# A list scheduler takes other engines' results to reach TensorE by a fixed margin later, and its costs are set anew

## Chip, core and metric

One core of a Trainium2 chip runs the whole program. The metric is the device time in microseconds of one execution.

## What is computed

Three stages follow each other on 2304 tokens (4 batches of 576): attention that keeps each row's 32 largest scores, an MLP with the gate h·cos(h), and a mixture of eight experts that all see every token and whose outputs are weighted by a matrix P, balanced in eight rounds.

```python
scores = scale * np.matmul(q, k.transpose(0, 1, 3, 2))
kth = np.partition(scores, -32, axis=-1)[..., -32:-31]
attn = softmax(np.where(scores >= kth, scores, -1e9)); x = attn @ v
h = x @ w_in; x = (h * np.cos(h)) @ w_out
P = exp(x @ w_gate); eight times: rows of P to sum 1, then columns, times N / E
out += P[:, e:e + 1] * (np.maximum(x @ w1[e], 0.0) @ w2[e])     # for each of 8 experts
```

w_in and w_out arrive as 64-bit numbers and are decoded on the core to 32-bit ones.

## The kernel before

Nothing is issued where it is written. Each `put` (L262) records an operation with its engine, a cost in ns, what it reads and writes, and a priority by engine and class of work (`PRIORITY`, L28). `Plan.issue` (L150) then runs a list scheduler: it keeps a time at which each engine is free, takes the earliest engine that has something ready, and gives it the ready operation with the smallest priority number. An operation is ready when all that it depends on has ended, plus a latency by the two engines (`LAT`, L75). The order in which operations are taken is the order in which they are issued, so the table of costs decides where every instruction stands in its engine's queue. Each engine then works through its queue strictly in that order and waits, where an input is late, with all that stands behind.

The work, in the order of the program:

- *Decode*: 32 blocks of weights. Per block two VectorE (DVE) operations (L325, L331), four ScalarE (ACT) and three GpSimd (POOL) ones (L330, L332, L333) that hand the data back and forth, and a transfer in and out.
- *First attention* and *first MLP*: 3 token tiles of batch 0, in plain fp32, beside the decode. An attention tile (`att_tile`, L436) is 128 rows of one head: scores in two halves through the one PSUM bank s (L447, L448, or L451 in the plain form), each copied out by ACT (L457); on DVE one MAX8 (L459), three rounds of MATCH_REPLACE8 and MAX8 (L464, L465) and a masked product (L466); small POOL operations (L460, L468, L470); then transposes of the weights `ex` on TensorE (PE) into the bank t, four and then one (L475), evacuated by ACT and DVE (L493, L494). Per head `att_out` multiplies by v (L501, L503), again in bank t. The third tile's gate (L588 to L595) leads to `x2fl` (L669), without which the experts' work can't start.
- *Attention* of all other tokens (batch 0, 1, 2, 3), whose buffers come free with the end of the decode, beside *fill*: the experts' two layers (`fill`, L762) for the 3 first tiles, later for 4 more. On PE attention has priority 2 and fill 3, so fill goes where attention is not ready.
- *moe1*: the first MLP for the other tokens, one part (512 tokens) after batch 1, three parts after batch 3.
- P (`sinkhorn`), then the experts for the other tokens, with products combined in pairs; to the end.

fp32 products are made of three matmuls of rounded parts (`mm3`, L370: high·high, high·low, low·high), so weights are split into `whi` and `wlo` on ACT and POOL (L345, L347).

Of the kernel before, what the change touches and what calls it, by code (L numbers as in the profile page):

```python
# [12 lines left out]
I32 = mybir.dt.int32  # L13
U32 = mybir.dt.uint32
AF = mybir.ActivationFunctionType
ALU = mybir.AluOpType
# [7 lines left out]
LOWEST = -3.0e38  # L24
# [12 lines left out]
class Buf:  # L37


    def __init__(self, plan, pool, shape, dtype, name):  # L40
        self.plan, self.pool, self.shape, self.dtype, self.name = plan, pool, shape, dtype, name
        self.tile = None
        self.log = []
# [27 lines left out]
class Plan:  # L71
# [6 lines left out]
        ("POOL", "ACT"): 69.0, ("POOL", "DVE"): 70.0, ("POOL", "POOL"): 96.0, ("PE", "SP"): 189.0, ("ACT", "SP"): 140.0,  # L78
        ("DVE", "SP"): 120.0, ("POOL", "SP"): 67.0, ("SP", "SP"): 10.0, ("SP", "PE"): 80.0, ("SP", "ACT"): 10.0, ("SP", "DVE"): 10.0, ("SP", "POOL"): 10.0,
    }  # L80

    def __init__(self, tc, pools):
        self.tc, self.pools = tc, pools
# [66 lines left out]
    def issue(self):  # L150
        ops = self.ops
        for op in ops:
            op.outs, op.left, op.ready = [], len(op.deps), 0.0
        for k, op in enumerate(ops):
            for d in op.deps:
                ops[d].outs.append(k)
        engines = ("PE", "ACT", "DVE", "POOL", "SP")
        soon = {e: [] for e in engines}
        now = {e: [] for e in engines}
        free = dict.fromkeys(engines, 0.0)  # L160
        dma_free, func, warm, window, busy = 0.0, None, False, -1, {}
        for k, op in enumerate(ops):
            if not op.left:
                heapq.heappush(soon[op.eng], (0.0, k))
        order = []
        while len(order) < len(ops):
            best = None
            for e in engines:
                if now[e]:
                    t = free[e]  # L170
                elif soon[e]:
                    t = max(free[e], soon[e][0][0])
                else:
                    continue
                if best is None or t < best[0]:
                    best = (t, e)
            t, e = best
            while soon[e] and soon[e][0][0] <= t:
                k = heapq.heappop(soon[e])[1]
                heapq.heappush(now[e], (ops[k].prio, k))  # L180
            k = heapq.heappop(now[e])[1]
            op = ops[k]
            cost = op.cost
            if op.func and op.func != func:
                cost, func = cost + 1283.0, op.func
            if e == "PE":
                w = int(t / 3413)
                if w != window:
                    past = busy.get(w - 1, 0.0) / 3413
                    warm = past > 0.95 or (warm and past > 0.5)  # L190
                    window = w
                cost *= 1.0 if warm else 2.0
                a = t
                while a < t + cost:
                    z = min(t + cost, (int(a / 3413) + 1) * 3413.0)
                    busy[int(a / 3413)] = busy.get(int(a / 3413), 0.0) + z - a
                    a = z
            free[e] = op.end = t + cost
            if e == "SP":
                dma_free = max(t + cost + 650.0, dma_free) + op.bytes / 360.0  # L200
                op.end = dma_free + 900.0
            order.append(k)
            for o in op.outs:
                n = ops[o]
                n.ready = max(n.ready, op.end + self.LAT.get((e, n.eng), 130.0))
                n.left -= 1
                if not n.left:
                    heapq.heappush(soon[n.eng], (n.ready, o))
        self.estimate = max(op.end for op in ops)
        for k in order:  # L210
            ops[k].emit()


def mm_ns(n):
    return max(107.0, n / 2.4 + 3.0)


def act_ns(n, psum=False, ap=False):
# [11 lines left out]
def fused_kernel(tc, kq, vv, w_in, w_out, w_gate, w1, w2, out, B=4):  # L230
# [4 lines left out]
    V, A_, G_, T_ = nc.vector, nc.scalar, nc.gpsimd, nc.tensor  # L235
# [26 lines left out]
    def put(eng, cost, emit, reads=(), writes=(), func=None, nbytes=0):  # L262
        return add(eng, cost, emit, reads, writes, PRIORITY[eng][CLASSES.index(work)], func, nbytes)
# [51 lines left out]
    def decode(src, keep, part):  # L315

        raw, mag, sgn, low = d_raw(), d_mag(), d_sgn(), d_low()  # L320
        dma(lambda: raw.ap, lambda: src.bitcast(I32), 1 << 19, writes=[raw])
        hi = lambda dt: raw.ap.bitcast(dt).rearrange("p (n t) -> p n t", t=2)[:, :, 1]
        lo = lambda: raw.ap.bitcast(U32).rearrange("p (n t) -> p n t", t=2)[:, :, 0]
        magf = lambda: mag.ap.bitcast(F32)
        put("DVE", 335, lambda: V.tensor_scalar(mag.ap, hi(I32), 3, 0x40000000, op0=ALU.logical_shift_left, op1=ALU.bitwise_xor), [raw], [mag])  # L325
        put("ACT", 613, lambda: A_.activation(sgn.ap, hi(F32), AF.Identity, bias=cols.ap[:, 1:2]), [raw, cols], [sgn])
        put("ACT", 613, lambda: A_.activation(sgn.ap, sgn.ap, AF.Sign, bias=cols.ap[:, 2:3]), [sgn, cols], [sgn])
        put("ACT", 520, lambda: A_.activation(low.ap, lo(), AF.Copy, scale=2.0**-52), [raw], [low])
        put("ACT", 520, lambda: A_.activation(magf(), magf(), AF.Abs), [mag], [mag])
        put("POOL", 1225, lambda: G_.tensor_tensor(magf(), magf(), sgn.ap, op=ALU.mult), [mag, sgn], [mag])  # L330
        put("DVE", 335, lambda: V.tensor_scalar(sgn.ap.bitcast(I32), mag.ap, -8388608, None, op0=ALU.bitwise_and), [mag], [sgn])  # L331
        put("POOL", 1225, lambda: G_.tensor_tensor(low.ap, low.ap, sgn.ap, op=ALU.mult), [low, sgn], [low])  # L332
        put("POOL", 1225, lambda: G_.tensor_tensor(low.ap, magf(), low.ap, op=ALU.add), [mag, low], [low])  # L333
        dma(keep, lambda: low.ap, 1 << 18, [low], [part])
# [101 lines left out]
    def att_tile(stats, dests, plain=None):  # L436
# [4 lines left out]
        sc, m, wk, ex = sc_r(), m_r(), wk_r(), ex_r()  # L441
# [16 lines left out]
        mc = lambda i, k=1: m.ap[:, i : i + k]  # L458
# [2 lines left out]
        put("ACT", act_ns(S, ap=True), lambda: A_.activation(ex.ap, sc.ap, AF.Exp, scale=0.125, bias=mc(32)), [sc, (m, 32, 33)], [ex], func="exp")  # L461
        for r in range(3):
            src = wk if r else sc
            put("DVE", 669, lambda r=r, src=src: V.match_replace(wk.ap, mc(8 * r, 8), src.ap, LOWEST), [src, (m, 8 * r, 8 * r + 8)], [wk])  # L464
            put("DVE", 669, lambda r=r: V.max(mc(8 * r + 8, 8), wk.ap), [wk], [(m, 8 * r + 8, 8 * r + 16)])  # L465
        put("DVE", 729, lambda: V.scalar_tensor_tensor(ex.ap, sc.ap, mc(31), ex.ap, op0=ALU.is_ge, op1=ALU.mult, accum_out=mc(33)),  # L466
            [sc, ex, (m, 24, 32)], [ex, (m, 33, 34)])
        put("POOL", 162, lambda: G_.tensor_scalar(mc(34), mc(33), 1e-9, 1.0, op0=ALU.add, op1=ALU.mult), [(m, 33, 34)], [(m, 34, 35)])  # L468
        put("DVE", 75, lambda: V.reciprocal(mc(35), mc(34)), [(m, 34, 35)], [(m, 35, 36)])  # L469
# [2 lines left out]
        for c0, c1, p in ((0, 4, 128), (4, 5, 64)):  # L472
# [8 lines left out]
            for r0, rn, hd, t0 in dests:  # L481
# [10 lines left out]
                hi, lo = (ath, 1000 * c0 + t0, 1000 * c0 + t0 + rn), (lb, 2000 * c0 + t0, 2000 * c0 + t0 + rn)  # L492
# [601 lines left out]
```

## Time and profile before

| | us |
|---|---|
| median of 3 runs (lowest, highest) | 2482.4 (2480.8, 2483.6) |
| the profiled execution | 2480.5 |
| its span, first to last instruction | 2478.7 |

The profile is of one execution. Its records give start and duration of each instruction; the page says that matmuls are pipelined and their ends modelled, so that the record of one overlaps the next. PEld is TensorE's loading of weights, which stands ahead of each matmul. A wait is the engine's idle time and the instruction that ended it. Row names in the fences further down are lines of the kernel before.

### The profile page before, as it was taken

What the parts mean: (1) busy time and instruction counts of PE and PEld (TensorE: products, weight loads), DVE (VectorE), ACT (ScalarE), POOL (GpSimd) and SP (SyncE); (2) the same over time, 40 slices, a digit from 0 to 9 for tenths busy, and PEclk for the clock granted to TensorE, in tenths of its full rate; (3) what the DMA queues carried; (4) which work ended last, traced back from release to release, by engine and by line L of the source; (5) the groups of instructions that cost most, each with busy time, mean ns of one, the idle gap of its engine ahead of it and who ended that gap; (6) DMA issues with size and microseconds to landing.
All of it is one profiled execution on the core that took longest, in us unless ns stands there. A gap on an engine that the chain in (4) does not pass through costs nothing.

```text
span 2478.7 us, 33516 instructions
## 1 busy us (share of the span) xinstructions
PE 2364.7 (95%) x11089; PEld 1905.7 (77%) x11089; DVE 1986.9 (80%) x3651; ACT 1271.7 (51%) x2438; POOL 1266.6 (51%) x1328
## 2 busy tenths in 40 slices
PE   6878999999889999999999999999999999999999
PEld 3434688888667877778878888788888888888887
DVE  8997599999998999999986787776666666666655
ACT  6785566666578666666566776322322222322221
POOL 6886487767577656656520033433443334443330
PEclk9889999999899999999999999999999999999999
DMA  8765654444323333333334333022222221111101
GB/s 263 232 210 186 200 167 144 139 123 151 109 74 97 114 115 115 115 119 97 97 114 123 91 108 104 27 64 81 81 85 81 73 60 35 36 42 43 35 22 47
DMA packets 159501, 261.37 MB, mean 105 GB/s; under 512 B 15008, under 2 KB 60656, under 8 KB 159328
## 3 DMA queue, kind: packets, MB, share of 16 engines
q1 hardware_dynamic: 159328, 259.24, 34.5%
q8 instruction: 87, 1.43, 0.2%
q14 instruction: 86, 0.70, 0.1%
HBM read 227.31 MB, written 31.87 MB: 105 GB/s over the span
## 4 chain that ended last, share of the span: by engine, by line
PE 57%; DVE 28%; POOL 6%; issue 4%; ACT 3%; DMA 1%; SPq 0%; POOLq 0%; ACTq 0%; DVEq 0%
PE y L372 9%; PE y L373 9%; PE y L374 9%; DVE wk L464 7%; DVE m L465 6%; DVE ex L466 4%; PE g L374 2%; PE g L373 2%; PE g L372 2%; DVE m L459 2%; POOL wlo L347 2%; DVE atl L494 1%; PE y L383 1%; PE y L387 1%; PE y L384 1%
## 5 line engine op out<-in xcount | busy, mean ns | idle before, releaser
L347 POOL TENSOR_TENSOR wlo<-raw,whi 128x512 fp32r<-128x512 f32 x336 | 451.7, 1349 | 195.1 <-ACT whi L345 116.3
L465 DVE MAX8 m<-wk 128x8 f32<-128x576 f32 x432 | 318.1, 748 | 1.9
L953 DVE SCALAR_TENSOR_TENSOR acc<-y,P,acc 128x512 f32<-128x512 f32 x308 | 229.2, 748 | 103.5 <-PE y L374 103.2
L345 ACT ACTIVATE whi<-raw 128x512 fp32r<-128x512 f32 x416 | 259.2, 627 | 96.5 <-PE y L374 36.9
L464 DVE MATCH_REPLACE8 wk<-m,wk 128x576 f32<-128x576 f32 x288 | 213.5, 742 | 1.1
L372 PE MATMUL y<-whi,gh 128*128 128x512 f32 x448 | 182.0, 406 | 0.0
L372 PE MATMUL y<-gh,xh 128*128 128x512 f32 x450 | 177.1, 393 | 1.0 <-DVE acc L949 1.0
L374 PE MATMUL y<-whi,gl 128*128 128x512 f32 x448 | 176.5, 394 | 0.0
L373 PE MATMUL y<-gl,xh 128*128 128x512 f32 x450 | 176.5, 392 | 0.0
L374 PE MATMUL y<-gh,xl 128*128 128x512 f32 x450 | 176.2, 392 | 0.0
L373 PE MATMUL y<-wlo,gh 128*128 128x512 f32 x448 | 176.0, 393 | 0.0
L475 PE MATMUL t<-ident,ex 128*128 128x128 f32 (+1 forms) x720 | 136.6, 290 | 39.7 <-POOL ex L470 10.9
L457 ACT ACTIVATE sc<-s 128x288 f32<-128x288 f32 x288 | 117.0, 406 | 95.6 <-DVE ex L466 54.9
L475 PEld LDWEIGHTS t<-ident,ex 128*128 128x128 f32 (+1 forms) x720 | 85.9, 140 | 101.6 <-POOL ex L470 27.8
L466 DVE SCALAR_TENSOR_TENSOR ex<-sc,m,ex 128x576 f32<-128x576 f32 x144 | 152.8, 1061 | 3.6 <-ACT ex L461 1.8
L470 POOL TENSOR_SCALAR ex<-ex,m 128x576 f32<-128x576 f32 x144 | 111.2, 772 | 33.9 <-DVE m L469 33.0
L493 ACT ACTIVATE ath<-t 64x128 fp32r<-64x128 f32 (+3 forms) x272 | 104.5, 396 | 46.2 <-PE t L475 40.0
L461 ACT ACTIVATE ex<-sc,m 128x576 f32<-128x576 f32 x144 | 111.3, 773 | 32.4 <-POOL m L460 31.4
L459 DVE MAX8 m<-sc 128x8 f32<-128x576 f32 x144 | 106.9, 743 | 9.2 <-ACT sc L457 9.1
L464 DVE MATCH_REPLACE8 wk<-m,sc 128x576 f32<-128x576 f32 x144 | 106.7, 741 | 0.0
L372 PEld LDWEIGHTS y<-gh,xh 128*128 128x128 f32 x450 | 85.2, 189 | 20.0 <-DVE acc L949 1.8
L372 PE MATMUL y<-gh,gh 128*128 128x512 f32 x254 | 99.4, 391 | 0.0
(376 smaller groups left out, 7054.6 us busy)
## 6 DMA issues: line engine op xcount, KB each, us to landing
raw<-in_w_dram SPq DMA_DIRECT2D x384, 256.0 KB, 2.6
kq<-in_kq_dram SPq DMA_DIRECT2D x32, 576.0 KB, 4.3
raw<-win_d SPq DMA_DIRECT2D x64, 256.0 KB, 3.0
raw<-wout_d SPq DMA_DIRECT2D x64, 256.0 KB, 2.7
y_d<-st SPq DMA_DIRECT2D x56, 256.0 KB, 3.0
raw<-y_d SPq DMA_DIRECT2D x56, 256.0 KB, 2.7
wp<-win_d SPq DMA_DIRECT2D x24, 512.0 KB, 5.3
wp<-wout_d SPq DMA_DIRECT2D x24, 512.0 KB, 4.4
```

The source lines that it names most:

```text
L345: put("ACT", act_ns(n), lambda: A_.activation(hv(), rv(), AF.Copy), [rb], [hb])
L347: put(e, c, lambda: f.tensor_tensor(lv(), rv(), hv().bitcast(F32), op=ALU.subtract), [rb, hb], [lb])
L372: T_.matmul(o(), ah(), bh(), start=start, stop=False)
L373: T_.matmul(o(), ah(), bl(), start=False, stop=False)
L374: T_.matmul(o(), al(), bh(), start=False, stop=stop)
L457: put("ACT", act_ns(288, psum=True), lambda c=c: A_.activation(sc.ap[:, c], o(), AF.Copy), [ps_s], [(sc, c.start, c.stop)])
L459: put("DVE", 669, lambda: V.max(mc(0, 8), sc.ap), [sc], [(m, 0, 8)])
L464: put("DVE", 669, lambda r=r, src=src: V.match_replace(wk.ap, mc(8 * r, 8), src.ap, LOWEST), [src, (m, 8 * r, 8 * r + 8)], [wk])
L465: put("DVE", 669, lambda r=r: V.max(mc(8 * r + 8, 8), wk.ap), [wk], [(m, 8 * r + 8, 8 * r + 16)])
L466: put("DVE", 729, lambda: V.scalar_tensor_tensor(ex.ap, sc.ap, mc(31), ex.ap, op0=ALU.is_ge, op1=ALU.mult, accum_out=mc(33)), [sc, ex, (m, ...
L475: T_.transpose(pt()[:p, c - c0, :], ex.ap[:, c * 128 : c * 128 + p], ident.ap)
L953: put("DVE", 663, lambda y=y, av=av, pcol=pcol: V.scalar_tensor_tensor(av(), y.ap, pcol(), av(), op0=ALU.mult, op1=ALU.add), [y, P, a], [a])
```

## The change

A constant `SLACK` of 600 ns is added to the time at which PE can take a result of another engine or of a transfer, in the planner's estimate only. The transfer rate of the estimate goes from 360 to 280 bytes per ns, a matmul's cost from n / 2.4 + 3.0 to n / 2.4 + 13.6 ns, and five DVE costs are raised. No operation, buffer, priority or wait is added or removed; only the order of issue differs. Lines of the new kernel are 4 higher than those of the kernel before.

```diff
+    SLACK = 600.0
...
             if e == "SP":
-                dma_free = max(t + cost + 650.0, dma_free) + op.bytes / 360.0
+                dma_free = max(t + cost + 650.0, dma_free) + op.bytes / 280.0
                 op.end = dma_free + 900.0
...
                 n = ops[o]
-                n.ready = max(n.ready, op.end + self.LAT.get((e, n.eng), 130.0))
+                n.ready = max(n.ready, op.end + self.LAT.get((e, n.eng), 130.0) + (self.SLACK if n.eng == "PE" != e else 0.0))
...
 def mm_ns(n):
-    return max(107.0, n / 2.4 + 3.0)
+    return max(107.0, n / 2.4 + 13.6)
...
-        put("DVE", 335, lambda: V.tensor_scalar(mag.ap, hi(I32), 3, 0x40000000, op0=ALU.logical_shift_left, op1=ALU.bitwise_xor), [raw], [mag])
+        put("DVE", 600, lambda: V.tensor_scalar(mag.ap, hi(I32), 3, 0x40000000, op0=ALU.logical_shift_left, op1=ALU.bitwise_xor), [raw], [mag])
...
-            put("DVE", 669, lambda r=r, src=src: V.match_replace(wk.ap, mc(8 * r, 8), src.ap, LOWEST), [src, (m, 8 * r, 8 * r + 8)], [wk])
+            put("DVE", 738, lambda r=r, src=src: V.match_replace(wk.ap, mc(8 * r, 8), src.ap, LOWEST), [src, (m, 8 * r, 8 * r + 8)], [wk])
...
-        put("DVE", 729, lambda: V.scalar_tensor_tensor(ex.ap, sc.ap, mc(31), ex.ap, op0=ALU.is_ge, op1=ALU.mult, accum_out=mc(33)),
+        put("DVE", 960, lambda: V.scalar_tensor_tensor(ex.ap, sc.ap, mc(31), ex.ap, op0=ALU.is_ge, op1=ALU.mult, accum_out=mc(33)),
```

(The decode's second DVE operation, L331, goes from 335 to 600 as the first does.)

What this does to the queues is shown at three places. The first is PE's queue in the second stretch of attention and fill, between a tile's last transpose (`t<-ident,ex`, 64x128) and the product with v (`t<-ath,vs`), which needs that transpose evacuated by ACT and DVE. Before:

```order
L475 MATMUL t<-ident,ex_223 64x128
L372 MATMUL g<-x2fh,whi_1687 128x512
L373 MATMUL g<-x2fl,whi_1687 128x512
L374 MATMUL g<-x2fh,wlo_1715 128x512
L372 MATMUL g<-x2fh,whi_1687 128x512
L373 MATMUL g<-x2fl,whi_1687 128x512
L374 MATMUL g<-x2fh,wlo_1715 128x512
L501 MATMUL t<-ath_1604,vs_1393 128x320
```

And now:

```order
L479 MATMUL t<-ident,ex_236 64x128
L376 MATMUL g<-x2fh,whi_1749 128x512
L377 MATMUL g<-x2fl,whi_1749 128x512
L378 MATMUL g<-x2fh,wlo_1764 128x512
L376 MATMUL g<-x2fh,whi_1749 128x512
L377 MATMUL g<-x2fl,whi_1749 128x512
L378 MATMUL g<-x2fh,wlo_1764 128x512
L376 MATMUL g<-x2fh,whi_1749 128x512
L377 MATMUL g<-x2fl,whi_1749 128x512
L378 MATMUL g<-x2fh,wlo_1764 128x512
L505 MATMUL t<-ath_1605,vs_1193 128x320
```

Three matmuls of fill more stand between the two. Over all such places of this stretch the product stands 10 rows behind (median of 27 places) before, 7 rows in 9 of them; now 12 rows (median of 26), 7 rows in one.

The second place is DVE's queue ahead of the first MLP's third gate (L590, now L594). Before:

```order
L669 TENSOR_TENSOR x2fl<-y_754,x2fh 128x4x128
L459 MAX m_127<-sc_115 128x8
L464 MATCH_REPLACE wk_134<-m_127,sc_115 128x576
L465 MAX m_127<-wk_134 128x8
L464 MATCH_REPLACE wk_134<-m_127,wk_134 128x576
L465 MAX m_127<-wk_134 128x8
L464 MATCH_REPLACE wk_134<-m_127,wk_134 128x576
L465 MAX m_127<-wk_134 128x8
L466 SCALAR_TENSOR_TENSOR ex_137,m_127<-sc_115,m_127,ex_137 128x576
L469 RECIPROCAL m_127<-m_127 128x1
L590 TENSOR_TENSOR rr_907<-rr_907,hs_718 128x1024
```

And now, the last rows ahead of it:

```order
L473 RECIPROCAL m_192<-m_192 128x1
L469 MAX m_213<-wk_140 128x8
L468 MATCH_REPLACE wk_140<-m_213,wk_140 128x576
L469 MAX m_213<-wk_140 128x8
L470 SCALAR_TENSOR_TENSOR ex_236,m_213<-sc_183,m_213,ex_236 128x576
L594 TENSOR_TENSOR rr_905<-rr_905,hs_856 128x1024
```

Before, 25 attention tiles stand ahead of this gate in DVE's queue, now 27: the two added ones are of the attention that needs the decode's end. On PE, 8 of that attention's score halves stand ahead of the first attention's last product with v, where 3 stood.

The third place is the decode's end in POOL's queue (its last row is L333, now L337). Before:

```order
L332 TENSOR_TENSOR d_low_177<-d_low_177,d_sgn_231 128x512
L333 TENSOR_TENSOR d_low_177<-d_mag_175,d_low_177 128x512
L470 TENSOR_SCALAR ex_223<-ex_223,m_127 128x576
L468 TENSOR_SCALAR m_169<-m_169 128x1
L460 TENSOR_SCALAR m_200<-m_200 128x1
```

And now:

```order
L336 TENSOR_TENSOR d_low_173<-d_low_173,d_sgn_208 128x512
L472 TENSOR_SCALAR m_135<-m_135 128x1
L337 TENSOR_TENSOR d_low_173<-d_mag_180,d_low_173 128x512
L474 TENSOR_SCALAR ex_202<-ex_202,m_135 128x576
L464 TENSOR_SCALAR m_213<-m_213 128x1
```

The decode's last row is the 176th of POOL's queue before and the 160th now; on DVE 20 attention tiles were complete ahead of the last decode operation, now 16. From the end of `sinkhorn` on, PE's last 3961 matmuls stand in the same order as before.

## Rows read from the trace of the kernel before

**Rows 1.** Busy us by window: PE, PEld, DVE, ACT, POOL (instructions), clock, DMA.

```profile
20.00:212.00 192.00, 156.82 (x500) 77.82 (x500) 187.85 (x342) 145.00 (x271) 164.07 (x164) 0.89 0.73 223
212.00:290.00 78.00, 69.46 (x263) 36.79 (x262) 37.52 (x76) 36.23 (x71) 29.38 (x36) 0.98 0.62 201
310.00:640.00 330.00, 323.47 (x1822) 287.25 (x1821) 322.87 (x719) 224.66 (x492) 254.71 (x295) 1.00 0.48 145
640.00:686.00 46.00, 33.35 (x142) 26.08 (x141) 45.14 (x103) 23.26 (x51) 23.16 (x34) 0.78 0.30 89
686.00:806.00 120.00, 105.14 (x493) 82.39 (x492) 108.60 (x176) 94.18 (x153) 88.16 (x78) 0.99 0.30 87
806.00:1250.00 444.00, 438.43 (x2212) 355.62 (x2211) 437.14 (x951) 272.07 (x577) 268.82 (x340) 1.00 0.37 110
1250.00:1612.00 362.00, 348.84 (x1625) 292.43 (x1624) 270.16 (x447) 219.97 (x367) 92.16 (x75) 0.99 0.32 95
1612.00:2418.00 806.00, 805.02 (x3665) 679.41 (x3664) 517.69 (x731) 222.26 (x389) 319.66 (x278) 1.00 0.19 57
```

**Rows 2.** DVE in order of time, 226 to 246 us: start, us, instruction, [idle before].

```profile
228.60 0.16 DVE L469 RECIPROCAL m<-m 128x1 f32<-128x1 f32 x1 [2.31 <-POOL m L468]
232.45 0.69 DVE L669 TENSOR_TENSOR x2fl<-y,x2fh 128x512 fp32r<-128x512 f32 x1 [3.69 <-ACT x2fh L668]
233.06 0.75 DVE L459 MAX8 m<-sc 128x8 f32<-128x576 f32 x1
...
239.61 0.08 DVE L466 DVE_READ_ACCUMULATOR ex<-sc,m,ex 128x1 f32 x1
...
245.63 1.22 DVE L590 TENSOR_TENSOR rr<-rr,hs 128x1024 f32<-128x1024 f32 x1 [5.46 <-POOL rr L589]
```

**Rows 3.** POOL by line, 20 to 212 us: busy us, mean ns, idle before.

```profile
L332 POOL TENSOR_TENSOR d_low<-d_low,d_sgn 128x512 f32<-128x512 f32 x32 | 45.8, 1431 | 10.2 <-DVE d_sgn L331 9.6
L333 POOL TENSOR_TENSOR d_low<-d_mag,d_low 128x512 f32<-128x512 f32 x32 | 44.1, 1379 | 1.4
L330 POOL TENSOR_TENSOR d_mag<-d_mag,d_sgn 128x512 f32<-128x512 f32 x31 | 41.9, 1363 | 0.1
L470 POOL TENSOR_SCALAR ex<-ex,m 128x576 f32<-128x576 f32 x20 | 16.4, 822 | 5.7 <-DVE m L469 5.6
L468 POOL TENSOR_SCALAR m<-m 128x1 f32<-128x1 f32 x21 | 5.1, 242 | 9.4 <-DVE ex L466 8.6
```

**Rows 4.** DVE's masked product by line: 20 to 212 us, then 310 to 640 us.

```profile
L466 DVE SCALAR_TENSOR_TENSOR ex<-sc,m,ex 128x576 f32<-128x576 f32 x21 | 27.5, 1309 | 0.0
...
L466 DVE SCALAR_TENSOR_TENSOR ex<-sc,m,ex 128x576 f32<-128x576 f32 x42 | 43.3, 1032 | 0.5
```

**Rows 5.** Waits of PE's weight loads, 806 to 1250 us: total us, times, longest.

```profile
PEld t L475 <- POOL ex L470: 7.3, 17, 1.0
PEld s L447 <- ACT sc L457: 6.4, 16, 1.4
PEld t L475 <- DVE atl L494: 5.4, 14, 0.9
```

**Rows 6.** Waits of PE's matmuls, 806 to 1250 us.

```profile
PE t L475 <- POOL ex L470: 1.8, 5, 0.5
PE s L447 <- ACT sc L457: 1.7, 3, 1.0
PE t L475 <- DVE x L509: 0.7, 1, 0.7
PE t L475 <- DVE atl L494: 0.7, 2, 0.4
```

**Rows 7.** A fill matmul by line, 806 to 1250 us: busy us, mean ns.

```profile
L374 PE MATMUL y<-whi,gl 128*128 128x512 f32 x240 | 94.5, 394 | 0.0
```

More of the change, by code (lines that the diff above doesn't have):

```diff
@@ L330, in decode @@
         put("POOL", 1225, lambda: G_.tensor_tensor(magf(), magf(), sgn.ap, op=ALU.mult), [mag, sgn], [mag])
-        put("DVE", 335, lambda: V.tensor_scalar(sgn.ap.bitcast(I32), mag.ap, -8388608, None, op0=ALU.bitwise_and), [mag], [sgn])
+        put("DVE", 600, lambda: V.tensor_scalar(sgn.ap.bitcast(I32), mag.ap, -8388608, None, op0=ALU.bitwise_and), [mag], [sgn])
         put("POOL", 1225, lambda: G_.tensor_tensor(low.ap, low.ap, sgn.ap, op=ALU.mult), [low, sgn], [low])
```

## Prediction

> **What bounds the kernel now.** First the span by windows [rows 1]: it falls into stages with different limits. In the first, 20 to 212 us (decode, first attention), DVE is busy for 187.85 of 192 us, PE only for 156.82, at a granted clock of 0.89: DVE sets the pace. From 212 to 290 us no engine does: DVE works for 37.52 of 78 us, while the third tile goes through the first MLP and fill waits for its result. From 310 to 640 us DVE (322.87 of 330) and PE (323.47) are both full. At 640 us fill has run out, and DVE alone finishes batch 1's attention (45.14 of 46 us, PE 33.35). From 806 to 1250 us both are full again (PE 438.43, DVE 437.14 of 444 us). After that PE alone decides: 348.84 of 362 us, and then 805.02 of 806.
>
> So there are three places where order can save time: the DVE idle before 290 us, DVE's small gaps up to 686 us, and PE's gaps from 806 to 1250 us. The last needs a second look, because PE's busy time hides gaps. A fill matmul's record lasts 394 ns [rows 7], while matmuls start every 444 / 2212 = 0.20 us [rows 1]; so a gap of up to some 0.19 us between two of them is covered by the record's tail. That is why the waits are read on the weight loads as well [rows 5] as on the matmuls [rows 6]: 7.3 + 6.4 + 5.4 = 19.1 us of weight loads that wait for the same three results, against 1.8 + 1.7 + 0.7 + 0.7 = 4.9 us on the matmuls.
>
> **The change, part by part.** No operation is added or taken away, so every term is a wait that goes or comes. The costs and the slack act only through the order; they are taken by the place in the queue that they move.
>
> *PE's cover in 806 to 1250 us.* The steps that wait are those at which an attention tile comes back to PE: the score bank after ACT's copy, the transposes after POOL's scaling, the next transposes after DVE's evacuation. Each of these now stands later, as the first place of the order shows: the median goes from 10 to 12 rows of fill between transposes and product with v, two to three rows of 0.20 us, some 0.5 us. The waits are short: 7.3 us in 17, 6.4 in 16, 5.4 in 14, that is 0.43, 0.40 and 0.39 us on average, 1.4 us at the longest [rows 5]. Cover of 0.5 us removes most of them. What they cost PE lies between 4.9 us [rows 6] and 19.1 us [rows 5]. As some 0.19 us of each wait is hidden in the matmuls' records, 47 waits hide up to 9 us, and I take 4.9 + 9 = 14 us as the real cost, nearer to the weight loads' rows. Two thirds of it go, the longest remain: -9.5 us. Can DVE follow? It has only 444 - 437.14 = 6.9 us idle in this stage [rows 1]. But attention needn't end before fill: the first layer of the next part needs no more attention than batch 2's first tiles, and the order now puts 108 of its matmuls ahead of the last product with v, where 36 stood. That is 72 more of 0.20 us or longer, some 15 us in which attention's tail has cover on PE. So I keep -9.5, with ends at 0 (DVE is late instead) and at -17 us (all the waits but 2 us of them).
>
> *DVE's hole before 290 us.* DVE idles for 78 - 37.52 = 40.5 us between 212 and 290 us [rows 1]. The second place of the order puts two more attention tiles ahead of the third gate. A tile's chain on DVE ran from 233.06 to 239.69 us [rows 2], 6.6 us, so 13.2 us of work are pulled into the hole. Up to the gate at 245.63 us the idle pieces are 2.31, 3.69 and 5.46 us [rows 2], together 11.5; the gate, and with it fill's start, comes 1.7 us later. Fill's later start costs nothing by itself: PE has 12.7 us to spare from 640 to 686 us [rows 1], and DVE still has attention to do. What counts is that DVE does batch 1's last tile earlier: 13.2 - 1.7 = 11.5 us gained at the start of moe1.
>
> *The price of that: a denser decode.* The two tiles can be there only because decode ends earlier. On POOL its end moves from the 176th row to the 160th, on DVE from behind 20 tiles to behind 16. Four tiles of 6.6 us less leave DVE 187.85 - 26.4 = 161 us of work up to the decode's end; POOL keeps 164.07 less four scalings of 0.82 us [rows 3], some 161 us. Before, POOL had 192 - 164.07 = 28 us in hand; now both queues are full at the same time, and POOL's 1431, 1379 and 1363 ns per decode operation [rows 3], which the table still holds for 1225, can't be caught up. Each engine waits for the other several times per block. How much DVE loses is not in the trace: at least nothing, at most POOL's whole 28 us. Of these 28, 9.6 + 8.6 = 18.2 are waits for DVE by two operations [rows 3], and they vanish where POOL is the late one; the other 9.8 remain. DVE will hide part of them; I take a loss of 7 us. Net of both: -4.5 us, with ends at -11.5 and +16.5.
>
> Here a rule of the Trainium skill speaks against the change. The row first: the masked product, which reads two SBUF inputs, takes 1309 ns beside the decode and 1032 ns beside fill [rows 4]. SBUF — State Buffer, section SBUF: two separate sides, says that such a VectorE operation and a GpSimd one that reads SBUF lock the same pair of ports for a whole instruction, and the other is blocked. By it the decode's rows grow with POOL's share: 277 ns at 164 / 192 = 85% busy would be 326 ns at 100%, over 16 tiles 0.8 us more. By the row alone the sum is as above, by the rule 1 us longer; I leave it out as too small.
>
> *DVE's gaps from 310 to 686 us.* DVE idles for 7.1 and 0.9 us [rows 1]. Better cover on PE delivers transposes and scores without stalls, but later by the slack; four score buffers stand between. I take -2 us, ends 0 and -6.
>
> *686 to 806 us, and all after 1250 us.* The same steps in nearly the same order; PE's order after sinkhorn is the old one, and PE is busy for 805.02 of 806 us there [rows 1]. Nothing, give or take 3 us.
>
> Transfer rate and slack move SP's queue too. No row of PE's waits [rows 5, 6] names a transfer, so I cost that at nothing; the cover is the five raw buffers, and if it failed, whole matmul groups would wait in front of a split weight.
>
> **The sum.** -9.5 - 4.5 - 2 = -16 us. The profiled execution took 2480.5 us (span 2478.7), so 2464.5; the median of the runs is 1.9 above it, so the forecast for the median is 2466 us.
>
> **Rivals.**
>
> *POOL becomes the bound of the decode, and it is slower.* Place: 20 to 212 us. DVE waits in its queue for d_mag and for the small POOL results, and the first attention behind them is late. It decides from the point where these waits cost more than the other gains, 9.5 + 2 + 11.5 = 23 us; where PE's gain too stays out, 13.5 us are enough. At the full 28 us, with half of PE's gain: 28 - 11.5 - 2 - 5 = +9.5 us, 2492 us. For it: both queues hold 161 us of work for the same stretch. Against it: POOL's waits now are mostly waits for DVE, which are harmless where POOL has the work. Chance 0.12.
>
> *DVE was the limit, and PE's waits only change places.* The removed PE waits become idle PE time at the end of attention, as DVE can give only 6.9 us [rows 1]. With 7 us lost in the decode: -4.5 - 2 and up to -2, and with 4 us more lost there, it is within 5 us: about 2478 us. For it: DVE is at 98% in both full stages. Against: moe1's matmuls now stand beside attention's tail. Chance 0.18.
>
> *The slack starves DVE.* A tile comes back to PE three times or more, so its scores and transposes arrive some 2 us later; if four score buffers don't carry that, DVE waits in each of the tiles from 310 to 1250 us. From 0.16 us in each of some 100 tiles it eats the whole gain of 16 us; at 0.5 us it is +50 - 16 = +34 us, 2516 us. Against it: the places in which PE's queue mixes tiles and fill hold the same number of tiles per stretch of fill. Chance 0.04.
>
> **How the numbers follow.** The forecast has the remaining 0.66, a gain of 5 us or more. A difference under 0.2%, 5 us, can't be told from none here. The range reaches from the sum with PE's waits all gone and the decode's price small (-17 - 9 - 6 = -32, 2450 us) to the first rival at 2 us short of its price (2490 us). Faster by over 0.2%: 0.66 and a share of the second rival, 0.70. Within: 0.16. Slower: 0.14.
>
> **What would show it.** Right: the weight loads' waits for ex, sc and atl in 806 to 1250 us fall from 19.1 to under 7 us; DVE is busy for some 50 of 78 us between the decode's old end and fill; moe1 starts 5 to 12 us earlier, at 675 to 681 us. Wrong on the decode: DVE's busy share in 20 to 180 us falls under 0.95, with waits for POOL's d_mag, m and d_low on it. Wrong on the slack: DVE waits for ACT's sc or for PE's transposes between 310 and 1250 us.

## The result, and the profile after

The changed kernel is slower: 2499.4 us (median of 4 runs, 2496.4 to 2500.8) against 2482.4 us (2480.8 to 2483.6), a ratio of 1.0067 (95% interval 1.0050 to 1.0085). The forecast was 2466 us with a range to 2490 us. The profiled execution took 2499.95 us, its span 2498.2 us, 19.5 us longer than before.

The same windows as [rows 1], of the changed kernel: stretch and its length, then busy us of PE, PEld, DVE, ACT and POOL with their instructions, granted clock, DMA share, GB/s.

```profile
20.00:212.00 192.00, 150.53 (x429) 76.30 (x429) 178.53 (x320) 137.18 (x261) 168.84 (x166) 0.80 0.66 211
212.00:290.00 78.00, 72.48 (x287) 39.00 (x287) 54.73 (x112) 42.66 (x77) 23.71 (x36) 0.98 0.65 210
310.00:640.00 330.00, 321.25 (x1807) 283.29 (x1808) 320.38 (x705) 222.08 (x491) 252.35 (x290) 1.00 0.49 143
640.00:686.00 46.00, 40.63 (x214) 34.14 (x212) 44.90 (x102) 28.22 (x62) 30.85 (x37) 0.96 0.45 135
686.00:806.00 120.00, 102.00 (x458) 79.48 (x456) 110.07 (x183) 89.69 (x146) 90.24 (x84) 0.96 0.28 82
806.00:1250.00 444.00, 440.52 (x2242) 364.53 (x2243) 437.93 (x958) 274.75 (x588) 272.86 (x341) 1.00 0.38 111
1250.00:1612.00 362.00, 341.23 (x1579) 285.79 (x1577) 262.96 (x420) 220.08 (x372) 89.61 (x74) 0.97 0.33 96
1612.00:2418.00 806.00, 804.29 (x3657) 677.86 (x3658) 542.96 (x756) 221.67 (x387) 310.81 (x277) 1.00 0.19 56
```

Three lines changed most for the worse: DVE in the first (178.53 busy, 187.85 before), PE from 686 to 806 us (102.00, 105.14 before), and PE from 1250 to 1612 us (341.23, 348.84 before). Two changed for the better as forecast: DVE is busy for 54.73 us from 212 to 290 us (37.52 before), and PE did 2242 matmuls from 806 to 1250 us in place of 2212.

**Where PE's time went.** Every kernel here has the same 11089 PE instructions, and PE sets the end. So the comparison is made in lost PE time. For each matmul of the kernel before, the lower quartile of the interval from its start to the next start, taken by line, output and shape, stands for its undisturbed time; what an interval holds above that is called lost. The undisturbed times add up to the same 2228 us in every kernel, so the differences of lost time add up to the difference of the end (to 0.3 us for the change). The stretches are of each kernel's own time; an interval that crosses a boundary can move an entry by 1 to 2 us to its neighbour, and the sum stays.

Lost PE time against the kernel before, us (the runs below the second line are explained in the next section; "ahead" is how many moe1 matmuls the order puts ahead of attention's last product with v):

| kernel | ahead | 0 to 310 | 310 to 640 | 640 to 686 | 686 to 806 | 806 to 1290 | 1290 to 1320 | 1320 to end | sum |
|---|---|---|---|---|---|---|---|---|---|
| lost in the kernel before | 36 | 116.7 | 21.2 | 22.8 | 22.1 | 28.0 | 0.8 | 28.3 | |
| the change | 108 | +16.1 | +3.7 | -13.6 | +6.7 | -7.8 | +14.6 | +0.1 | +19.8 |
| slack alone | 108 | +11.5 | +3.6 | -6.6 | +11.5 | -4.6 | +9.4 | +6.3 | +31.1 |
| costs alone | 3 | +17.4 | +7.6 | -17.8 | +6.8 | +4.7 | -0.7 | +3.9 | +21.9 |
| first stage old, rest new | 108 | +0.5 | -0.6 | +7.1 | +1.4 | -5.8 | +10.0 | +4.6 | +17.2 |
| first stage new, rest old | 0 | +16.1 | +3.4 | -19.5 | -0.4 | -1.6 | -0.6 | -1.2 | -3.8 |
| change, no slack 210 to 690 | 81 | +13.2 | +6.8 | -14.1 | +8.3 | -4.2 | +4.4 | -0.8 | +13.6 |
| change, short ring | 114 | +11.3 | +4.6 | -11.6 | +4.1 | -7.8 | -0.7 | -2.0 | -2.1 |
| slack for batch 2, fill | 0 | +16.8 | +2.4 | -19.6 | +2.9 | -2.0 | -0.7 | -2.2 | -2.4 |
| late slack, short ring | 96 | +17.0 | +3.4 | -19.5 | +2.6 | -12.2 | -0.8 | -4.1 | -13.6 |
| before, short ring | 36 | +0.4 | -1.1 | 0.0 | +0.9 | -1.2 | -0.8 | -3.6 | -5.4 |
| slack for batch 0 too | 36 | +12.7 | +1.7 | -10.7 | +0.9 | -2.0 | 0.0 | -1.7 | +0.9 |
| late slack, old start, short ring | 117 | +0.2 | -0.9 | -1.1 | -3.0 | -8.4 | -0.7 | -1.8 | -15.7 |
| late slack 1200, short ring | 252 | +15.8 | +4.2 | -21.6 | +5.3 | +9.0 | +8.8 | +2.8 | +24.3 |

For the change the table says: up to 310 us it loses 16.1 us (its granted clock of 0.80, 0.89 before, is in that), of which 640 to 686 us gives 13.6 back, since fill no longer runs out there; 806 to 1290 us gains 7.8; and 14.6 us are lost in one stretch of 30 us, from 1290 to 1320 us.

**That stretch.** PE's waits of the changed kernel, 1250 to 1330 us (us in total, times, longest):

```profile
PE y L387 <- ACT ch L349: 3.8, 1, 3.8
PE t L479 <- DVE atl L498: 2.0, 1, 2.0
PE t L505 <- DVE x L513: 1.0, 1, 1.0
PE t L505 <- DVE ath L498: 0.9, 1, 0.9
```

ACT in order of time, 1296 to 1316 us (start, us, instruction, [idle before]):

```profile
1306.83 0.43 ACT L512 ACTIVATE avt<-t 64x320 f32<-64x320 f32 x1 [3.30 <-PE t L505]
1310.64 0.43 ACT L512 ACTIVATE avt<-t 64x320 f32<-64x320 f32 x1 [3.38 <-PE t L505]
1313.75 0.63 ACT L349 ACTIVATE ch<-raw 128x512 fp32r<-128x512 f32 x1 [2.67 <-DMA x_d<-x]
```

PE can't begin moe1's second layer (y, L387) before the weights are split into `ch`. `ch` and `cl` are the sixth pair of weight buffers, added to the ring for the last three moe1 parts, and they lie in the pool `ph2`, which takes over attention's memory. So the split waits for the transfer of attention's last result (x_d<-x). In the kernel before, attention ended in time: nothing waited for ch. Now 108 matmuls of the first layer stand ahead of attention's last product; that product starts at 1307.8 us, and PE, ACT and DVE all idle for it. The gaps of PE's records in the stretch add up to 8.3 us; most of the rest goes with the granted clock, 0.73 on average there, so for a part of it the lower level of 1.2 GHz, after PE had stood idle: the 128x512 matmuls start 0.43 us apart at 1317 us and 0.23 us apart at 1293 us.

**The weight loads' waits**, 806 to 1250 us, which answer to [rows 5]:

```profile
PEld s L451 <- ACT sc L461: 4.2, 8, 1.1
PEld t L479 <- DVE atl L498: 2.1, 2, 2.0
PEld t L479 <- DVE x L513: 1.8, 4, 0.7
```

The wait for ex is gone; sc and atl are left with 6.3 us of the 19.1.

### The profile page after: what moved, and what is told of

Its sections match the earlier page's. It is cut to its first block, busy times and chain, and to the rows that moved or that the text cites. A ratio compares the mean times of both kernels' runs of the same rounds, so it can differ in the third digit from the quotient of the medians.

```text
span 2498.2 us, 33482 instructions
## 1 busy us (share of the span) xinstructions
PE 2375.0 (95%) x11089; PEld 1918.5 (77%) x11089; DVE 2013.1 (81%) x3651; ACT 1267.2 (51%) x2438; POOL 1262.2 (51%) x1328
## 3 DMA queue, kind: packets, MB, share of 16 engines
q1 hardware_dynamic: 159328, 259.24, 34.6%
## 4 chain that ended last, share of the span: by engine, by line
PE 60%; DVE 19%; ACT 3%; POOL 3%; issue 2%; DMA 0%; POOLq 0%; ACTq 0%; DVEq 0%
PE y L376 9%; PE y L377 9%; PE y L378 9%; DVE wk L468 4%; DVE m L469 4%; PE g L376 2%; PE g L378 2%; PE g L377 2%; DVE ex L470 2%; PE t L479 1%; PE h L376 1%; PE h L377 1%; PE h L378 1%; PE y L387 1%; PE y L388 1%
## 5 line engine op out<-in xcount | busy, mean ns | idle before, releaser
L351 POOL TENSOR_TENSOR wlo<-raw,whi 128x512 fp32r<-128x512 f32 x336 | 457.6, 1366 | 187.6 <-ACT whi L349 122.7
L463 DVE MAX8 m<-sc 128x8 f32<-128x576 f32 x144 | 106.9, 744 | 10.8 <-ACT sc L461 10.7
L376 PEld LDWEIGHTS y<-gh,xh 128*128 128x128 f32 x450 | 84.5, 188 | 19.8 <-issue 1.1
```

The lines of the kernel that those rows point to most:

```text
L351: put(e, c, lambda: f.tensor_tensor(lv(), rv(), hv().bitcast(F32), op=ALU.subtract), [rb, hb], [lb])
L376: T_.matmul(o(), ah(), bh(), start=start, stop=False)
```

## The experiments

Two theories at the start: *D and T* (the dense decode delays all that follows by 11.5 us at moe1's start; attention's tail costs 13 us), and *S* (the slack feeds DVE late in every stage).

**Slack alone.** Costs and transfer rate of the kernel before, `SLACK = 600.0`.

```diff
-                dma_free = max(t + cost + 650.0, dma_free) + op.bytes / 280.0
+                dma_free = max(t + cost + 650.0, dma_free) + op.bytes / 360.0
...
-    return max(107.0, n / 2.4 + 13.6)
+    return max(107.0, n / 2.4 + 3.0)
```

(and the five DVE costs set back.)

> The slack of 600 ns alone; transfer rate and all costs as in the kernel before. In the order, the decode's last POOL operation stands at row 170 (172 before, 156 with the whole change), so the decode is nearly as loose as before; 108 first-layer matmuls of the next moe1 part stand ahead of attention's last product with v, as with the whole change. Theory D+T (the dense decode starts the first stage's results about 19 us late, 11.5 us of it left at moe1's start; and attention's tail behind 108 matmuls costs about 13 us, while PE's cover from 806 to 1250 us gives back 11): no loss in the decode, the other two remain, 2482 - 11 + 13 = about 2484 us, moe1's start within 4 us of the kernel before. Rival S (the slack feeds DVE late in every stage, and that is the whole loss): 2495 us or more.

Measured: 2511.4 us, ratio 1.0123 (1.0108 to 1.0138); moe1's first gate 23.5 us later than before. **Costs alone** is the counterpart (the transfer rate goes with the costs; no run changes it by itself):

```diff
-    SLACK = 600.0
+    SLACK = 0.0
```

> The changed costs and transfer rate alone, slack 0. The decode's last POOL operation stands at row 160, nearly as with the whole change; only 3 first-layer matmuls stand ahead of attention's last product with v. Theory D+T: the decode's loss of about 11 us at moe1's start is there, PE's waits on weight loads from 806 to 1250 us stay near 19 us, the tail costs nothing: 2491 to 2494 us. Rival S: without slack nothing is late, 2480 to 2485 us.

Measured: 2496.7 us, 1.0066 (1.0051 to 1.0081). Both parts of the change are slower by themselves, by 30 and 16 us; together they cost 17: they are orders, not costs that add up. The tail behaves as T says (9.4 us lost with 108 matmuls ahead, nothing with 3), and the gain from 806 to 1290 us is there only with the slack. The run of the slack alone lies where S had it, but S alone falls, since without any slack 14 us are lost ahead of 806 us as well, and costs alone are far above its 2480 to 2485 us. The slack alone missed D and T too: moe1 started late though the decode's last POOL operation stood where it had been but for two rows.

**First stage old, rest new**, and **first stage new, rest old**. An operation carries a mark, set while decode, first attention and first MLP are recorded; those are planned with the old costs and no slack (the second run: they alone with the new ones).

```diff
+        pl.early = work in ("first attention", "first mlp", "decode")
...
-                n.ready = max(n.ready, op.end + self.LAT.get((e, n.eng), 130.0) + (self.SLACK if n.eng == "PE" != e else 0.0))
+                n.ready = max(n.ready, op.end + self.LAT.get((e, n.eng), 130.0) + (self.SLACK if n.eng == "PE" != e and not n.early else 0.0))
```

> The whole change, but the decode, the first attention and the first MLP are planned with the old costs and without slack (transfer rate 360 throughout); up to the third gate the order on PE, DVE and POOL is that of the kernel before, after it slack and new costs hold, and 108 matmuls stand ahead of attention's last product. Theory D+T: moe1 starts at 684 to 688 us as before, the loss of 11.5 us there is gone, the tail's 13 us remain: 2499.4 - 11.5 = about 2488 us. If the dense decode is not the cause (rival S), it stays at 2495 us or more.

> The counterpart: only the decode, the first attention and the first MLP are planned with slack and new costs (transfer rate 280 throughout); all other work with the old costs and without slack. The order up to the third gate is that of the whole change; no moe1 matmul stands ahead of attention's last product. Theory D+T: the decode's loss alone, moe1 starts about 11 us late, 2482.4 + 11 = about 2493 us. Rival S: with the slack gone from attention, fill and moe1 it is 2480 to 2486 us.

Measured: 2494.4 us, 1.0054 (1.0037 to 1.0070), and 2475.4 us, 0.9980 (0.9970 to 0.9989). Both miss theory D. The dense decode is there in the second run, with the same 16.1 us of lost PE time up to 310 us, but the kernel is faster than before. The lost time all comes back from 640 to 686 us, where PE had idled before. What decides there is when DVE has finished batch 1: its last tile (taken at its reciprocal on DVE) came at 645.8 us in this run, 656.5 before, 663.1 with the change. (The expectations count from 0.27 us later, so that they have 645.5 and 662.8 for these times.) And this run filled DVE's hole. DVE's windows from 212 to 310 us, in the order: the kernel before, the change, this run.

```profile
212.00:310.00 98.00, 88.57 (x371) 53.53 (x371) 55.63 (x117) 51.10 (x107) 48.04 (x58) 0.98 0.62 196
212.00:310.00 98.00, 90.29 (x352) 49.70 (x351) 62.59 (x131) 49.65 (x94) 32.34 (x45) 0.97 0.63 199
212.00:310.00 98.00, 87.92 (x357) 48.11 (x357) 75.87 (x160) 52.65 (x105) 36.54 (x54) 1.00 0.62 200
```

DVE is idle for 42.4, 35.4 and 22.1 us. The new theory, *H*: the decode's price is met in the hole, and what keeps attention's tiles out of the hole is lost.

**What closes the hole.** First the change without slack from the attention of batch 0 to the first moe1 part:

```diff
+    pl.slack = 0.0
     attention(0, LEAD)
...
+    pl.slack = pl.SLACK
     moe1(Part(n0, two, keep_parts(x2fh, x2fl)), 3)
```

> The whole change, but without slack for all that is recorded from the attention of batch 0 up to the first part of moe1, that is attention of batches 0 and 1 and fill of the first three tiles; costs and transfer rate as changed. The decode's last POOL operation at row 156 and the order to the third gate as with the change; 81 moe1 matmuls ahead of attention's last product. The four runs before this one changed the theory: the first stage in the new order ends at 2475 us with the rest old. Theory H (the dense decode's loss is given back where DVE's hole at 212 to 310 us is filled, and it is the slack that keeps attention's tiles out of the hole): DVE idle from 212 to 310 us falls from 35 us to 22 to 27, batch 1's last tile comes at 645 to 650 us (662.8 with the change), moe1's first gate at 688 to 692 us, and the time is 8 to 10 us under the change, 2489 to 2492 us; the tail's loss of 10 to 14 us at 1290 to 1320 us stays. Rival C (the hole stays open by the raised costs of the five DVE operations, not by the slack): DVE idle 33 us or more, time 2496 to 2500 us.

```profile
212.00:310.00 98.00, 89.75 (x353) 50.50 (x352) 63.43 (x131) 49.96 (x98) 33.60 (x48) 0.97 0.60 191
```

Measured: 2496.5 us, 1.0063 (1.0046 to 1.0079). DVE is busy for 63.43 of the 98 us, idle 34.6: with the raised costs in place, taking the slack away doesn't let the tiles into the hole, as rival C had it (which of the raised costs keeps them out, DVE's or the matmul's, wasn't tried). Then the opposite, the run of 2475.4 us with the slack for batch 0 added. The edit is shown on the form of that kernel in which each operation carries its own slack; the slack goes to 0 one line later:

```diff
-    pl.slack = 0.0
     attention(0, LEAD)
+    pl.slack = 0.0
```

> The run with the first stage as in the change and the rest old (2475.4 us), with one edit: the attention of batch 0 is planned with the slack of 600 ns too. In the order 28 attention tiles are complete on DVE ahead of the third x2fl, as with the change, where that run had 30; 36 moe1 matmuls stand ahead of attention's last product, where it had 0. Theory H (what is kept out of DVE's hole is lost): DVE idle from 212 to 310 us 33 us or more (22.1 in that run, 35.4 with the change), batch 1's last tile at 655 to 663 us (645.5 in that run), PE's loss to 806 us 6 to 12 us higher, time 2482 to 2488 us. Rival N (DVE's hole doesn't matter, as PE makes up for it): 2473 to 2478 us.

```profile
212.00:310.00 98.00, 90.50 (x358) 51.08 (x357) 61.61 (x126) 49.17 (x95) 33.62 (x46) 0.97 0.62 196
640.00:686.00 46.00, 40.51 (x201) 33.31 (x200) 44.66 (x99) 28.46 (x61) 31.48 (x39) 0.90 0.44 126
```

Measured: 2481.7 us, 1.0005 (0.9995 to 1.0014), 6.3 us more than without that edit. DVE is idle for 36.4 us (22.1 without), batch 1's last tile comes at 658.8 us (645.8 without), and 640 to 686 us gives PE only 10.7 us back, not 19.5. So H holds in DVE's idle time and in the tile; the time and PE's loss up to 806 us (5.0 us higher, though the first stage lost 3.4 us less in this execution) lie a little under what it had named. Either part of the change is enough to close the hole to attention's tiles: the slack by this run, the raised costs by the one before.

**The tail.** The change with one edit, the ring not made longer:

```diff
     ring = whi_r.bufs, wlo_r.bufs
-    whi_r.bufs, wlo_r.bufs = ring[0] + more[:1], ring[1] + more[1:]
```

> The whole change, but the three moe1 parts of the end don't add the sixth pair of weight buffers, ch and cl, to the ring; nothing else differs, and 114 moe1 matmuls stand ahead of attention's last product. Theory T (PE stands at 1290 to 1320 us because the second layer's weights are to be split into ch, whose pool takes the memory of attention's and can't be written before attention has ended): the wait of y for ch is gone, PE's loss of 15 us at 1290 to 1320 us falls to 2 to 4, time about 2486 to 2489 us. Rival T2 (PE stands there since the tail's matmuls themselves wait for DVE and ACT, which still have attention's last tiles to finish, whatever buffers the weights take): 2497 us or more, PE's loss there 10 us or more.

The stretch from 1290 to 1320 us, first with the change, then with the short ring:

```profile
1290.00:1320.00 30.00, 21.65 (x76) 16.37 (x75) 15.24 (x27) 12.62 (x24) 0.00 (x0) 0.73 0.14 41
1290.00:1320.00 30.00, 30.00 (x142) 25.20 (x141) 23.08 (x38) 20.19 (x34) 0.00 (x0) 1.00 0.35 103
```

Measured: 2479.5 us, 0.9995 (0.9985 to 1.0004), that is 19.9 us less than with the change by the medians. Attention's last result is no earlier (1313.5 us, 1311.1 with the change), 114 matmuls stand ahead of its product, and PE loses nothing: the second layer starts at 1285.0 us in place of 1314.4. T2 falls, T holds, and the time is lower than T's 2486 to 2489 us. The stretch itself is 15.3 us of it; 4.6 us are in the first stage, up to 212 us, though the orders of the two kernels are the same there. What differs is the granted clock from 180 to 212 us, first with the change, then with the short ring:

```profile
180.00:212.00 32.00, 29.88 (x88) 14.90 (x88) 25.65 (x58) 17.29 (x37) 23.59 (x28) 0.68 0.46 140
180.00:212.00 32.00, 30.07 (x108) 15.73 (x109) 30.25 (x68) 21.98 (x44) 26.52 (x31) 0.84 0.54 171
```

Eight of the kernels here have this order of the first stage, and their profiled executions go by that clock: three at 0.68 (the change is one) lose 15.7 to 16.3 us of PE time more than the kernel before up to 212 us, four at 0.79 lose 12.6 to 13.1, and the short ring's at 0.84 loses 11.7. So up to 4.6 us of the change's loss there vary from execution to execution of one order; why the clock differs stays open. The tail itself follows the number ahead: with the longer ring PE loses 9.4 to 14.6 us from 1290 to 1320 us with 108 matmuls ahead, 4.4 with 81, nothing with 36 or fewer.

The control is the kernel before with the same edit:

> The kernel before with one edit: the three moe1 parts of the end don't add ch and cl to the ring of weight buffers. 36 moe1 matmuls stand ahead of attention's last product, as before. Theory T (the late buffer costs only where the second layer comes within reach before attention has ended, which it did by 108 matmuls with the change): no wait of y for ch stood in the trace of the kernel before, so no difference, 2477 to 2485 us. Rival R (a shorter ring is better by itself, and the 20 us that the short ring gave the changed kernel have nothing to do with the order): 2460 to 2470 us.

Measured: 2475.0 us, 0.9980 (0.9969 to 0.9991). Neither expectation: it gains 5 us, of which the table shows 3.6 after 1320 us and 1.2 from 806 to 1290 us. So the short ring has a small worth of its own, whose cause wasn't tried, and a large one in the new order.

**Slack only where it pays.** The run of 2475.4 us with slack for batch 2 and the second fill; then with slack for batches 2 and 3 and the second fill, and the short ring; then that with the old first stage and the old costs (so the kernel before with two edits). The edits of the second are shown; the first sets the slack back to 0 ahead of `attention(3)` and leaves the ring:

```diff
+    pl.slack = pl.SLACK
     for b in range(2, B):
         attention(b)
     for e in range(NE):
         fill(e, LEAD, 4, two)
+    pl.slack = 0.0
...
-    whi_r.bufs, wlo_r.bufs = ring[0] + more[:1], ring[1] + more[1:]
```

> The run with the first stage as in the change and the rest old (2475.4 us), and the slack of 600 ns added for attention of batch 2 and for the second fill; attention of batch 3 and moe1 have none. No moe1 matmul stands ahead of attention's last product. Theory H+T: PE's loss from 806 to 1250 us falls by some 5 us, that at 1290 to 1320 us stays under 1 us: 2469 to 2472 us. Rival S (slack feeds DVE late wherever it is): 2475 us or more.

> The run with the first stage as in the change and the rest old (2475.4 us), and the slack added for attention of batches 2 and 3 and the second fill, with the ring of weight buffers not made longer; 96 moe1 matmuls stand ahead of attention's last product. Theory T by the buffer: the whole gain from 806 to 1250 us (some 8 us) is kept, 2466 to 2470 us. Rival T2: the gain is lost again at the tail, 2476 to 2482 us.

> The kernel before with the slack of 600 ns for attention of batches 2 and 3 and for the second fill alone, and with the ring of weight buffers not made longer; costs, transfer rate and the whole first stage as before. 117 moe1 matmuls ahead of attention's last product. It is the run of 2466.6 us with the old first stage. Theory P (slack late on covers PE's waits, 7 to 10 us between 806 and 1250 us, and with the short ring the tail costs nothing): 2470 to 2475 us, so that the new first stage is worth 4 to 8 us by itself. Rival D (the dense decode of the new first stage is a loss in every company): 2455 to 2463 us.

Measured: 2478.7 us, 0.9991 (0.9982 to 1.0001); 2466.6 us, 0.9940 (0.9925 to 0.9955); 2464.4 us, 0.9935 (0.9920 to 0.9950). The first lies where rival S had it: from 806 to 1290 us it loses 2.0 us less than the kernel before, but 1.6 of these were gone without that slack, and from 686 to 806 us it loses 3.3 us more than without; that DVE was fed late is not shown. The other two show the cover: the last one is 10.6 us under the short ring alone (2475.0 us), from which it differs by the late slack only. The last one also settles the first stage. With the hole filled, the new first stage is worth 2.2 us less than the old one, within what can be told: it is neither the loss that theory D made of it nor the gain of my theory P. This kernel, **the one before with slack from batch 2 on and a ring of five, beats both the kernel before and the change**.

**More slack.** The run of 2466.6 us with 1200 ns:

```diff
-    pl.slack = pl.SLACK
+    pl.slack = 1200.0
     for b in range(2, B):
```

> The run of 2466.6 us (first stage as in the change, slack for attention of batches 2 and 3 and the second fill, short ring) with the slack at 1200 ns in place of 600. 252 moe1 matmuls ahead of attention's last product, where it had 96. Theory P: the weight loads' waits from 806 to 1250 us are nearly gone with 600 already (some 5 us left), so it is the same within 3 us, 2464 to 2470 us. Rival S (more slack feeds DVE later): DVE's idle time from 806 to 1250 us grows past 20 us and the time past 2473 us.

With 600 ns from 806 to 1250 us, then with 1200 ns, there and from 1250 to 1320 us:

```profile
806.00:1250.00 444.00, 443.27 (x2251) 367.54 (x2250) 429.78 (x943) 270.87 (x577) 272.69 (x338) 1.00 0.37 113
...
806.00:1250.00 444.00, 443.96 (x2220) 367.32 (x2221) 411.07 (x870) 264.81 (x557) 266.66 (x325) 1.00 0.38 118
1250.00:1320.00 70.00, 51.03 (x207) 39.61 (x206) 64.01 (x128) 36.73 (x68) 9.37 (x20) 0.78 0.15 44
```

Measured: 2504.2 us, 1.0092 (1.0077 to 1.0107). Here S is right. PE stays full to 1250 us, but with fill; DVE is starved (idle 32.9 us, 14.2 with 600 ns), fill runs out, and attention's last tile comes at 1360 us, where it had come at 1260. The price appears later than its cause: PE then idles for DVE.

## Why the prediction was wrong

- *PE's cover, -9.5 us.* Right: 7.8 us less lost from 806 to 1290 us, the weight loads' waits at 6.3 us (forecast: under 7), and DVE followed, busy for 437.93 us of 444.
- *"But attention needn't end before fill."* **This step failed, and it is the largest: +14.6 us.** The 108 matmuls ahead of attention's last product were read as cover for attention's tail. They are, but attention's end stands behind them: its last result came 19.2 us later (1311.1 us, 1291.9 before), 7.8 us of which DVE's last tile brought with it (1276.3 us, 1268.5 before), and the second layer's sixth weight buffer lies in attention's memory. The prediction put all after 1250 us at nothing. What was missing is to name what is queued behind the moved instructions and who waits for their end. It stood in the code (`ph2` opens after `att`), and no row of the kernel before showed it, since there nothing waited.
- *DVE's hole, -11.5 us, and the denser decode, +7 us.* Net -4.5 and another -2 up to 686 us were forecast; batch 1's last tile came 6.6 us later. By DVE's idle time: +9.3 us from 20 to 212 us (13.5, 4.2 before), -7.0 from 212 to 310 us, +2.5 from 310 to 640 us, and 1.5 us of dearer work and small differences. The first of these has about the size of the decode's term, but only a part of its reason. Up to 180 us, close to the decode's end (DVE's last decode operation starts at 186.4 us), DVE idles only 3.4 us more than before; the other 5.9 us lie from 180 to 212 us, where DVE waits for the first MLP's gates for 4.1 us and PE runs at a granted clock of 0.68 (1.00 before), after it had been busy for 120.65 of the 160 us up to 180 us (130.25 before). At 0.84, in the same order, DVE idles there for 1.8 us and not for 6.4. And the hole took in less than the two tiles promised. The tiles fill small waits (25.2 us of them before from 212 to 310 us, 16.8 now), but the two long ones stay. Before:

```profile
267.35 0.69 DVE L494 TENSOR_TENSOR atl<-t,ath 128x512 fp32r<-128x512 f32 x1 [8.73 <-ACT ath L493]
...
284.00 0.69 DVE L669 TENSOR_TENSOR x2fl<-y,x2fh 128x512 fp32r<-128x512 f32 x1 [8.42 <-ACT x2fh L668]
```

And now:

```profile
285.79 0.69 DVE L498 TENSOR_TENSOR atl<-t,ath 128x512 fp32r<-128x512 f32 x1 [9.63 <-ACT ath L497]
...
303.00 0.69 DVE L673 TENSOR_TENSOR x2fl<-y,x2fh 128x512 fp32r<-128x512 f32 x1 [9.02 <-ACT x2fh L672]
```

They only moved, the second one past 290 us, where the prediction's window ends. So its sign for the hole came true (busy for some 50 of 78 us; 54.73 measured), and moe1's first gate still came 11.4 us later (698.0 us, 686.6 before) and not 5 to 12 us earlier. The run of 2475.4 us, with two tiles more ahead of the third x2fl, has no such wait for it.
- *"Fill's later start costs nothing by itself: PE has 12.7 us to spare."* Right: fill started 20.8 us later and PE got 13.6 us back from 640 to 686 us.
- *686 to 806 us, "nothing, give or take 3 us."* Measured +6.7 us. The runs don't tell why: kernels without slack on the moe1 part of this stretch lie between -3.0 and +6.8, kernels with it between +1.4 and +11.5, and the short ring's run, with the change's order up to 1289 us, at +4.1. This stays open.
- *The sum.* Up to 686 us +6.2 (forecast -6.5), then +6.7 (0), -7.8 (-9.5), +14.6 (0): +19.7 us in place of -16.
- *The rivals.* "POOL becomes the bound" had the right sign, and DVE's waits for POOL grew, but DVE's busy share from 20 to 180 us was 152.88 of 160 us, 0.96, above the 0.95 set as its mark. "The slack starves DVE" didn't happen in the change (DVE idles for 6.1 us from 806 to 1250 us, 6.9 before) and did at 1200 ns. None of the three named the tail.
- *The rule on the shared port* was weighed on the wrong instruction. See the last section.

## What to carry to other kernels

When an order changes, follow each stretch that now ends later to the buffers that its memory is handed on to: a wait that the old trace doesn't show may only have been met in time. Slack in a planner should cover the engine that is late, where it is late, and no more: 600 ns from batch 2 on gained 10 us (with the short ring), everywhere they lost 30 (with the longer one), and 1200 ns starved the other engine. Before pricing a stage's loss, look for the idle time behind it that will give it back; here 16 us lost by PE were worth nothing or 6 us, according to when another engine was done.

## What the runs showed of the hardware

DVE by line, 20 to 212 us: busy us, mean ns, idle before; before, then after.

```profile
L331 DVE TENSOR_SCALAR d_sgn<-d_mag 128x512 int32<-128x512 int32 x31 | 26.5, 854 | 2.1 <-POOL d_mag L330 2.0
L325 DVE TENSOR_SCALAR d_mag<-d_raw 128x512 int32<-128x512 int32 x28 | 22.4, 801 | 1.2 <-POOL d_low L333 1.2
```

```profile
L469 DVE MAX8 m<-wk 128x8 f32<-128x576 f32 x58 | 42.3, 744 | 0.0
L335 DVE TENSOR_SCALAR d_sgn<-d_mag 128x512 int32<-128x512 int32 x31 | 34.9, 1127 | 3.2 <-POOL d_mag L334 3.2
L329 DVE TENSOR_SCALAR d_mag<-d_raw 128x512 int32<-128x512 int32 x28 | 23.3, 833 | 0.8 <-POOL d_low L337 0.8
L470 DVE SCALAR_TENSOR_TENSOR ex<-sc,m,ex 128x576 f32<-128x576 f32 x18 | 19.7, 1093 | 0.0
```

The decode's second DVE operation became 273 ns dearer, while the masked product, 1309 ns before [rows 4], became cheaper. One piece of the changed kernel shows both lengths, DVE first and then POOL:

```profile
89.41 1.48 DVE L335 TENSOR_SCALAR d_sgn<-d_mag 128x512 int32<-128x512 int32 x1
90.81 0.75 DVE L469 MAX8 m<-wk 128x8 f32<-128x576 f32 x1
91.48 1.09 DVE L335 TENSOR_SCALAR d_sgn<-d_mag 128x512 int32<-128x512 int32 x1
92.49 0.41 DVE L329 TENSOR_SCALAR d_mag<-d_raw 128x512 int32<-128x512 int32 x1
```

```profile
87.40 3.20 POOL L334 TENSOR_TENSOR d_mag<-d_mag,d_sgn 128x512 f32<-128x512 f32 x2
91.02 1.27 POOL L336 TENSOR_TENSOR d_low<-d_low,d_sgn 128x512 f32<-128x512 f32 x1
```

An operation that starts while POOL has nothing under way takes 0.41 us; beside a POOL operation it takes up to 1.49 us; the first one here ends 0.3 us after POOL's pair. Of the 32 d_sgn operations, 22 started beside POOL in the kernel before (mean 1.04 us) and 29 in the changed one (mean 1.18 us); the others took 0.41 us in both. Of the masked products of the first 240 us, which take 0.81 us free and 1.5 to 1.6 us on average beside POOL, it was 15 of 25 and then 8 of 24. MAX8 took 744 ns in both kernels.

The Trainium skill, SBUF — State Buffer, section SBUF: two separate sides, names both kinds: VectorE operations with two SBUF inputs, and those in a two-port performance mode, contend with GpSimd for a pair of ports that one of them holds for a whole instruction. VectorE: DVE Perf Modes, section Mode 2×_2P, adds that an operation with one source in SBUF can use both read ports, even in fp32. The trace agrees, with 0.41 and up to 1.49 us. The prediction had applied the rule to the masked product alone and got 0.8 us; the 1032 ns that it took as the product's price without the decode are no free price either, as the product takes 0.81 us when it starts with POOL idle. The d_sgn operations alone are 32 times 264 ns (means of 841 and 1105 ns over all 32), 8.4 us, of which the masked products give some 4 us back; that these 4 us are part of the decode's loss follows from the records, and no run changed the contention by itself.
